# ScalarE's rounding copy of each dense weight half queued behind its first step for the next half

## The chip, the cores and the metric

The kernel runs on one core of a Trainium2 chip. The metric is the device time of one execution in microseconds (us). A core has TensorE (PE; PEld is its loading of weights), VectorE (DVE), ScalarE (ACT), GpSimd (POOL) and SyncE (SP), whose queue issues most of the transfers here. Each engine takes its own instructions in order, and semaphores tie the engines together.

## The reference, cut to what matters

Three layers on 2,304 tokens of width 512:

```python
# attention with random features: 4 batches, 8 heads, 576 tokens, head width 64, 128 features
h = x @ omega.T - sum(x*x)/2;  phi = exp(h - max(h)) / sqrt(m)        # for q and for k, scaled
num = phi_q @ (phi_k.T @ v);   den = phi_q @ sum(phi_k) + 1e-6;   x = num / den
# a dense layer: w_in is 512 x 2048, w_out is 2048 x 512
h = x @ w_in;  x = maximum(0.01*h, h) @ w_out
# eight experts, each token to the one with the largest logit
e = argmax(x @ w_gate);  out = gate * eom * (relu(x @ w1[e]) @ w2[e])
```

All of it is in 32-bit floats, except that `w_in` and `w_out` come in as 64-bit floats and are turned into 32-bit ones on the chip.

## The kernel before, in words

Each large product is made of three matmuls on numbers split in two: a high part, which is the value rounded to the type that TensorE multiplies fast (names ending in h: `xh`, `wih`, `woh`, `gh`), and a low part, the rest (`xl`, `wil`, `wol`, `gl`). The product is high by high, low by high, and high by low.

The tokens are cut into nine chunks of 256, the inner width of 2,048 into eight units of 256. `h_unit(c, u)` makes one unit of the hidden layer of chunk c (24 matmuls, lines 464 to 466), copies it out of PSUM (`g`, ScalarE line 469 and VectorE line 470) and splits it. `x_unit(c, u)` multiplies it with `w_out` (lines 483 to 485). Units of chunks 0 and 1 alternate. The attention items, in stages (`s_load` to `s_xt`), run ahead of the dense layer and then between its units: projection `pw` (line 291), row maxima and `bias` on VectorE (lines 303 to 312), `exp` on ScalarE (line 320), the sum over k (`kvp`, line 359, copied out by ScalarE as `kv`, line 374), transposes and `num` (lines 404 and 417), and the result `xr`, turned and split into `xh` and `xl`.

The dense weights come in 32 halves (`load_w`, line 174): for each unit u two of `w_in` and two of `w_out`, 512 KB each. A half is loaded into one of two `wraw` buffers (lines 184 and 196). ScalarE's **first step** (line 201) brings the upper word's exponent into range; three VectorE steps (lines 202 to 204) assemble the 32-bit float in `w32`, one of two buffers; ScalarE's **rounding copy** (line 209, in `hi_lo`) writes the high part; GpSimd's subtract (line 212) writes the low part. Eight halves (units 0 and 1) are loaded during the attention that goes ahead of the dense layer; the four of unit u+1 are asked for as chunk 0's unit u begins (line 829), for u from 1 to 6.

The order on each engine is set by a scheduler at build time: it simulates the program with estimated times, and takes from what is ready by priority, which is mostly the order in the text. `tc.issue_after(ins)` makes what is written in its block stand behind `ins` on the engine of `ins`. So one line that moves work can shift other instructions on every engine.

Of the kernel before, what the change touches and what calls it, by code (L numbers as in the profile page):

```python
# [11 lines left out]
F32 = mybir.dt.float32  # L12
# [3 lines left out]
AF = mybir.ActivationFunctionType  # L16
# [66 lines left out]
def f32(ap):  # L83
    return ap.bitcast(F32)
# [3 lines left out]
def tile_kernel(ctx: ExitStack, tc: tile.TileContext, kT, k_nat, v_nat, qT, q_nat, om, w_in, w_out, wg, w1, w2, out, stop=None, dbg=None):  # L88
    nc = tc.nc
# [45 lines left out]
    with ExitStack() as pa:  # L135
# [38 lines left out]
        def load_w(kind, u, half, pool):  # L174

            raw = pool.tile([P, 512, 2], I32, name="wraw", tag="wraw")
            if kind == "in":
                if win[u] is None:
                    wh = wring.tile([P, ND, 2 * P], F32R, name="wih", tag="w")
                    wl = wring.tile([P, ND, 2 * P], F32R, name="wil", tag="w")  # L180
                    win[u] = (wh, wl)
                wh, wl = win[u]
                with tc.issue_after(newest[-1]):
                    nc.sync.dma_start(raw.rearrange("p (i a) b -> p i (a b)", i=2),
                                      w_in[2 * half * P:2 * (half + 1) * P, u * 256:(u + 1) * 256].bitcast(I32).rearrange("(i p) a -> p i a", i=2))
                wh, wl = wh[:, 2 * half:2 * half + 2, :], wl[:, 2 * half:2 * half + 2, :]
                wh, wl = wh.rearrange("p a b -> p (a b)"), wl.rearrange("p a b -> p (a b)")
            else:
                if wout[u] is None:
                    wh = wring.tile([P, 2, D], F32R, name="woh", tag="w")  # L190
                    wl = wring.tile([P, 2, D], F32R, name="wol", tag="w")
                    wout[u] = (wh, wl)
                wh, wl = wout[u]
                f = 2 * u + half
                with tc.issue_after(newest[-1]):
                    nc.sync.dma_start(raw.rearrange("p a b -> p (a b)"), w_out[f * P:(f + 1) * P, :].bitcast(I32))
                wh, wl = wh[:, half, :], wl[:, half, :]
            top, low = raw[:, :, 1], raw[:, :, 0]
            w = pool.tile([P, 512], I32, name="w32", tag="w32")

            nc.scalar.activation(w.bitcast(F32), top.bitcast(F32), AF.Copy, scale=2.0 ** -112)
            nc.vector.tensor_scalar(w, w, 0x0FFFFFFF, 3, op0=ALU.bitwise_and, op1=ALU.logical_shift_left)
            nc.vector.scalar_tensor_tensor(w, top, -0x80000000, w, op0=ALU.bitwise_and, op1=ALU.bitwise_or)
            nc.vector.scalar_tensor_tensor(w, low, 29, w, op0=ALU.logical_shift_right, op1=ALU.bitwise_or)
            hi_lo(wh, wl, w.bitcast(F32), nc.scalar, nc.gpsimd)

        def hi_lo(dst_hi, dst_lo, src, hi_eng, lo_eng):
            if hi_eng is nc.scalar:
                nc.scalar.copy(dst_hi, src)
            else:  # L210
                hi_eng.tensor_copy(dst_hi, src)
            return lo_eng.tensor_sub(dst_lo, src, f32(dst_hi)).ins  # L212


        order = [(k, u, h) for u in range(NU) for k in ("in", "out") for h in range(2)]
        loaded = 0
# [238 lines left out]
        def h_unit(c, u):  # L455
            assert xdone.get(c) == CH * NH // 2, (c, u, xdone)
            hdone[c] = u + 1
            xh, xl = xT[c]
            hp = ps_h.tile([P, 2, CH], F32, name="hp", tag="h")
            wh, wl = win[u]  # L460
            for i in range(2):
                for d in range(ND):
                    a, b_ = wh[:, d, i * P:(i + 1) * P], wl[:, d, i * P:(i + 1) * P]
                    nc.tensor.matmul(hp[:, i, :], a, xh[:, d, :], start=d == 0, stop=False)  # L464
                    nc.tensor.matmul(hp[:, i, :], a, xl[:, d, :], start=False, stop=False)  # L465
                    nc.tensor.matmul(hp[:, i, :], b_, xh[:, d, :], start=False, stop=d == ND - 1)  # L466
            with tc.high_priority(offset=AHEAD):
                g = sb.tile([P, 2, CH], F32, name="g", tag="g", bufs=1)
                last_g[:] = [nc.scalar.copy(g, hp).ins]  # L469
                nc.vector.scalar_tensor_tensor(g, hp, 0.01, g, op0=ALU.mult, op1=ALU.max)  # L470
                gh = sb.tile([P, 2, CH], F32R, name="gh", tag="gh")
                gl = sb.tile([P, 2, CH], F32R, name="gl", tag="gl")
                last_g.append(hi_lo(gh, gl, g, nc.vector if c > 1 else nc.scalar, nc.vector))
            return gh, gl

        def x_unit(c, u, gg, acc):
            gh, gl = gg
            wh, wl = wout[u]
            for i in range(2):
                for t in range(2):  # L480
                    a, b_ = gh[:, i, t * P:(t + 1) * P], gl[:, i, t * P:(t + 1) * P]
                    h_, l_ = wh[:, i, :], wl[:, i, :]
                    nc.tensor.matmul(acc[t], a, h_, start=u == 0 and i == 0, stop=False)  # L483
                    nc.tensor.matmul(acc[t], a, l_, start=False, stop=False)  # L484
                    nc.tensor.matmul(acc[t], b_, h_, start=False, stop=u == NU - 1 and i == 1)  # L485
# [333 lines left out]
        for i, (c, u) in enumerate(pairs):  # L819

            rate = RATE
            for cc in range(c, NCH):
                left = [k + TAIL for k, it in enumerate(seq) if it[0] == cc] + [len(o) for c_, o in flow if c_ == cc]
                if left and hbeg.get(cc, 0) - 1 > i:
                    rate = max(rate, max(left) / (hbeg[cc] - 1 - i))
            if u == 0:
                at = [(ps_x, "x"), (ps_x, "x")] if c != 1 else [(ps_proj, "pj"), (ps_a, "a")]
                acc[c] = [ps.tile([P, D], F32, name=f"acc{t}", tag=tag) for t, (ps, tag) in enumerate(at)]
            while c == 0 and loaded < min(len(order), max(4 * (u + 2), WPRE + int(u * (32 - WPRE) / WU))):
                load_w(*order[loaded], wst)  # L830
                loaded += 1
            if i + 1 < len(pairs):
                gg[pairs[i + 1]] = h_unit(*pairs[i + 1])
            if c == NCH - 1 and u == 0:

                assert not flow and slot is not None
                pq.close()
                eo = ctx.enter_context(tc.tile_pool(name="eo", bufs=2, side="right", reuse_waits="tile"))
                block, second = Block(slot, 0), Block(slot, 1)
                block.rows()  # L840
                second.rows()
            owed += rate
            steps = int(owed)
            owed -= steps
            for k in range(steps + 1):
                if k == (steps + 1) // 2:
                    x_unit(c, u, gg.pop((c, u)), acc[c])
                if k == steps:
                    break
                if routes:  # L850
                    tick((-1, routes.pop(0)))
                elif seq and (seq[0][0] < 3 or i + int(6 / rate) >= hend.get(seq[0][0] - 2, 0)):
                    tick(seq.pop(0))
                else:
                    tick()
            if slot is None and c == NCH - 2 and not routes and not any(c_ < 0 for c_, _ in flow):
                slot = early()
                slot.fetch(0)
                slot.fetch(1)
            if c == NCH - 1:  # L860
                slot.split(u, last_g)
                if u == NU - 2:
                    for d in range(ND):
                        block.xt(d)
            if u < NU - 1:
                continue
            if c == 0:
                pads()
                gates()
            both_done[0] = c > 0  # L870
            rows = (wst if c == 1 else rt).tile([P, 2, ROW], F32, name="rows", tag="wraw" if c == 1 else "rows")
            nc.vector.memset(rows[:, :, D + 1:D + 2], 0.0)
            nc.scalar.copy(rows[:, 0, 0:D], acc[c][0])
            nc.vector.tensor_copy(rows[:, 1, 0:D], acc[c][1])
            routes.append(route_item(c, rows)[0])
# [138 lines left out]
```

## Time and profile before

| | |
|---|---|
| time, median of 3 runs | 862.88 us (862.8 to 868.14) |
| the profiled execution | 862.73 us, of which the span from the first to the last instruction is 861.0 us |
| busy in the span | PE 831.8 us (97%), DVE 450.7 (52%), ACT 306.5 (36%), POOL 176.1 (20%) |
| DVE busy by fortieths of the span, tenths | 6899788735555456445555444536644444243220 |
| TensorE clock granted, same slices | 9899899999999999999999999999999999999998 |

The 32 first steps start between 11.7 and 159.3 us, so the stretch in question is the first fifth of the span. The table shows averages over very different stages: what a change there is worth is read from the instructions for which TensorE waits in that stretch.

In the rows below, a row of the timeline gives the start, the duration, the engine, the line, the operation with its tiles as output<-inputs, and the number of instructions. The brackets tell how long the engine sat idle just before, and which instruction ended that.

### The profile page before, as it was taken

To read this page: it belongs to the slowest core of one execution; us is meant where nothing else is said; L and a number is where in the kernel's file an instruction comes from. 1 tells how busy PE (TensorE), PEld (TensorE's weight loads), DVE (VectorE), ACT (ScalarE), POOL (GpSimd) and SP (SyncE) were. 2 spreads that over 40 slices of the span, in tenths; PEclk is the share of its full clock that TensorE was granted. 3 is DMA by queue.
4 is the path that set the end of the run, shared out by engine and by line. 5 is a ranking of instruction groups with operands and counts; after the bars stand their busy time and mean duration, and the time that the engine had idled before them with its cause. 6 is when DMAs were issued, how large, how long until landed. Compare 5 with 4: busy or idle time off the path is not lost. (4 is left out here: it accounts for less than half of the span.)

```text
span 861.0 us, 13985 instructions
## 1 busy us (share of the span) xinstructions
PE 831.8 (97%) x5299; PEld 729.0 (85%) x5299; DVE 450.7 (52%) x1142; ACT 306.5 (36%) x755; POOL 176.1 (20%) x253
## 2 busy tenths in 40 slices
PE   9889988999999999999999999999999999999996
PEld 7768776788889988988889989898889789887894
DVE  6899788735555456445555444536644444243220
ACT  4666556434333323333333213214333334232210
POOL 3545544400122011112101010021003221120001
PEclk9899999899999999999999999999999999999998
DMA  7636655301443003133101000042505554151001
GB/s 230 208 120 185 190 179 166 124 10 31 60 81 102 26 26 56 46 71 76 43 27 24 2 25 2 10 121 74 98 26 179 177 155 123 59 172 50 7 25 33
DMA packets 46153, 73.55 MB, mean 85 GB/s; under 512 B 6017, under 2 KB 28673, under 8 KB 46082
## 3 DMA queue, kind: packets, MB, share of 16 engines
q1 hardware_dynamic: 42562, 63.14, 26.5%
q0 software_dynamic: 3520, 9.47, 3.5%
q8 instruction: 44, 0.72, 0.4%
q14 instruction: 27, 0.22, 0.1%
HBM read 62.00 MB, written 10.59 MB: 84 GB/s over the span
## 5 line engine op out<-in xcount | busy, mean ns | idle before, releaser
L464 PE MATMUL hp<-xh,wih 128*128 128x256 f32 x576 | 166.3, 289 | 2.3 <-DVE xl L212 2.0
L465 PE MATMUL hp<-xl,wih 128*128 128x256 f32 x576 | 161.8, 281 | 0.1
L466 PE MATMUL hp<-xh,wil 128*128 128x256 f32 x576 | 161.6, 281 | 0.0
L483 PE MATMUL acc<-woh,gh 128*128 128x512 f32 x288 | 123.0, 427 | 1.3 <-ACT kv L374 1.3
L320 ACT ACTIVATE h<-pw,bias 128x128 f32<-128x128 f32 x288 | 84.8, 372 | 105.7 <-DVE bias L312 81.5
L470 DVE SCALAR_TENSOR_TENSOR g<-hp,g 128x512 f32<-128x512 f32 x72 | 49.6, 689 | 135.8 <-ACT g L469 123.6
L485 PE MATMUL acc<-woh,gl 128*128 128x512 f32 x288 | 115.5, 402 | 0.0
L484 PE MATMUL acc<-wol,gh 128*128 128x512 f32 x288 | 114.3, 397 | 0.0
L464 PEld LDWEIGHTS hp<-xh,wih 128*128 128x128 f32 x576 | 108.8, 189 | 5.7 <-issue 2.4
L465 PEld LDWEIGHTS hp<-xl,wih 128*128 128x128 f32 x576 | 108.8, 189 | 2.1 <-DVE xl L212 0.3
L466 PEld LDWEIGHTS hp<-xh,wil 128*128 128x128 f32 x576 | 108.7, 189 | 0.0
L469 ACT COPY g<-hp 128x512 f32<-128x512 f32 x72 | 42.3, 587 | 138.3 <-PE hp L466 138.2
L723 PE MATMUL eht<-exh,ewh 128*128 128x256 f32 (+1 forms) x256 | 75.9, 296 | 0.0
L724 PE MATMUL eht<-exl,ewh 128*128 128x256 f32 (+1 forms) x256 | 75.6, 295 | 0.0
L725 PE MATMUL eht<-exh,ewl 128*128 128x256 f32 (+1 forms) x256 | 75.5, 295 | 0.0
L291 PE MATMUL pw<-om_raw,xpair 128*128 128x256 f32 (+1 forms) x260 | 71.8, 392 | 2.6 <-ACT h L320 2.6
L271 POOL TENSOR_TENSOR nat<-nat 128x256 f32<-128x256 f32 (+1 forms) x65 | 44.9, 693 | 135.9 <-DMA nat<-k_nat 58.8
L485 PEld LDWEIGHTS acc<-woh,gl 128*128 128x128 f32 x288 | 54.4, 189 | 12.7 <-DVE gl L212 0.5
L483 PEld LDWEIGHTS acc<-woh,gh 128*128 128x128 f32 x288 | 54.2, 188 | 12.5 <-ACT kv L374 1.7
L741 PE MATMUL eyt<-ewh,ehh 128*128 128x512 f32 (+1 forms) x160 | 64.6, 404 | 0.0
L727 DVE SCALAR_TENSOR_TENSOR ehl<-eht,ehh 128x256 fp32r<-128x256 f32 (+1 forms) x64 | 29.1, 456 | 67.2 <-ACT ehh L726 64.3
L742 PE MATMUL eyt<-ewl,ehh 128*128 128x512 f32 (+1 forms) x160 | 63.3, 395 | 0.0
(157 smaller groups left out, 1475.1 us busy)
## 6 DMA issues: line engine op xcount, KB each, us to landing
eraw<-w SPq DMA_DIRECT2D x32, 512.0 KB, 3.6
wraw<-w_in SPq DMA_DIRECT2D x16, 512.0 KB, 5.1
wraw<-w_out SPq DMA_DIRECT2D x16, 512.0 KB, 3.9
x_d<-rows SPq DMA_DIRECT2D x9, 514.0 KB, 8.9
xpair<-qT SPq DMA_DIRECT2D x18, 256.0 KB, 2.9
nat<-q_nat SPq DMA_DIRECT2D x30, 128.0 KB, 2.8
nat<-k_nat SPq DMA_DIRECT2D x27, 128.0 KB, 2.2
xpair<-kT SPq DMA_DIRECT2D x12, 256.0 KB, 6.2
```

The source lines that it names most:

```text
L291: nc.tensor.matmul(pj[:, 2 * j:2 * j + k // HD, :], st["raw"][0:k, j * P:(j + 1) * P], om_raw[0:k, 0:M * k // HD], start=True, stop=True)
L320: nc.scalar.activation(h[:, j, :], src[:, j // 2, j % 2], AF.Exp, bias=bias[:, j:j + 1], scale=sc)
L464: nc.tensor.matmul(hp[:, i, :], a, xh[:, d, :], start=d == 0, stop=False)
L465: nc.tensor.matmul(hp[:, i, :], a, xl[:, d, :], start=False, stop=False)
L466: nc.tensor.matmul(hp[:, i, :], b_, xh[:, d, :], start=False, stop=d == ND - 1)
L483: nc.tensor.matmul(acc[t], a, h_, start=u == 0 and i == 0, stop=False)
L484: nc.tensor.matmul(acc[t], a, l_, start=False, stop=False)
L485: nc.tensor.matmul(acc[t], b_, h_, start=False, stop=u == NU - 1 and i == 1)
L723: nc.tensor.matmul(t, wh, self.xh[:, d, 0:n], start=d == 0, stop=False)
L724: nc.tensor.matmul(t, wh, self.xl[:, d, 0:n], start=False, stop=False)
L725: nc.tensor.matmul(t, wl, self.xh[:, d, 0:n], start=False, stop=d == ND - 1)
L741: nc.tensor.matmul(t, a, wh, start=f == 0, stop=False)
```

## The change

Before, each `load_w` ended with the rounding copy and the subtract of its own half. Now it puts them on a list (`owing`), and the next `load_w` writes them right behind its own first step, with `issue_after`, so that on ScalarE the copy of half k stands behind the first step of half k+1. After the last half, a call in the main loop writes what is still owed. No instruction is added or removed, no buffer or transfer is changed.

```diff
-            nc.scalar.activation(w.bitcast(F32), top.bitcast(F32), AF.Copy, scale=2.0 ** -112)
+            first_ = nc.scalar.activation(w.bitcast(F32), top.bitcast(F32), AF.Copy, scale=2.0 ** -112).ins
+
+            parts_of_last(first_)
             nc.vector.tensor_scalar(w, w, 0x0FFFFFFF, 3, op0=ALU.bitwise_and, op1=ALU.logical_shift_left)
             ...
-            hi_lo(wh, wl, w.bitcast(F32), nc.scalar, nc.gpsimd)
+            owing.append((wh, wl, w.bitcast(F32)))
+
+        owing = []
+
+        def parts_of_last(after=None):
+            while owing:
+                with ExitStack() as order_:
+                    if after is not None:
+                        order_.enter_context(tc.issue_after(after))
+                    hi_lo(*owing.pop(0), nc.scalar, nc.gpsimd)
             ...
                 load_w(*order[loaded], wst)
                 loaded += 1
+            if c == 0 and loaded == len(order):
+                parts_of_last()
```

What the scheduler makes of it is seen in the engines' queues. In the changed kernel all lines behind 205 stand 11 to 13 lower in the file (209 is 220, 212 is 223, 320 is 331, 374 is 385, 469 is 480, 470 is 481), and the numbers of the tiles are smaller by two (`w_733` is `w_731`). Of the 32 halves, 16 had their copy behind the next half's first step already; for 15 the two now change places, and the last is as it was.

The first place is the end of the attention that goes ahead of the dense layer, at the first `g`. ScalarE's queue there before:

```order
L209 CAST woh<-w_733 128x512
L469 COPY g<-hp 128x512
L320 ACTIVATE h<-pw,bias 128x128 x4
L209 CAST gh<-g 128x512
L320 ACTIVATE h<-pw,bias 128x128 x4
L469 COPY g<-hp 128x512
L201 ACTIVATE w_904<-wraw 128x512
```

and now:

```order
L480 COPY g<-hp 128x512
L331 ACTIVATE h<-pw,bias 128x128 x4
L220 CAST gh<-g 128x512
L331 ACTIVATE h<-pw,bias 128x128 x4
L480 COPY g<-hp 128x512
L201 ACTIVATE w_902<-wraw 128x512
L220 CAST woh<-w_731 128x512
```

The copy of the eighth half has gone from ahead of the first `g` to behind the second `g` and the ninth half's first step. On VectorE at the same place, before:

```order
L303 TENSOR_REDUCE mx<-pw 128x2x2
L156 CAST wgo<-wg_raw 128x4x16
L310 SCALAR_TENSOR_TENSOR ngm<-mx,s_829 128x4
L470 SCALAR_TENSOR_TENSOR g<-hp,g 128x512
L312 TENSOR_TENSOR bias<-ngm,s_829 128x4
```

and now:

```order
L314 TENSOR_REDUCE mx<-pw 128x2x2
L481 SCALAR_TENSOR_TENSOR g<-hp,g 128x512
L321 SCALAR_TENSOR_TENSOR ngm<-mx,s_827 128x4
L283 TENSOR_REDUCE ssq<-nat 128x4
L323 TENSOR_TENSOR bias<-ngm,s_827 128x4
L156 CAST wgo<-wg_raw 128x4x16
```

The step for `g` now stands ahead of the cast of the gate's weights (`wgo`).

The second place is ScalarE around the last half of unit 3 (`w_1119`), before:

```order
L209 CAST woh<-w_1119 128x512
L469 COPY g<-hp 128x512
L374 COPY kv_1159<-kvp 128x132
L320 ACTIVATE h<-pw,bias 128x128 x3
L209 CAST gh<-g 128x512
L320 ACTIVATE h<-pw,bias 128x128
L201 ACTIVATE w_1310<-wraw 128x512
```

and now:

```order
L331 ACTIVATE h<-pw,bias 128x128 x7
L480 COPY g<-hp 128x512
L385 COPY kv_1157<-kvp 128x132
L201 ACTIVATE w_1308<-wraw 128x512
L220 CAST woh<-w_1117 128x512
L220 CAST gh<-g 128x512
```

The copies of `g` and `kv` no longer stand behind the copy of this half.

The third place is ScalarE around the second `w_in` half of unit 5 (`w_1534`), before:

```order
L201 ACTIVATE w_1534<-wraw 128x512
L209 CAST wih<-w_1525 128x512
L209 CAST wih<-w_1534 128x512
L320 ACTIVATE h<-pw,bias 128x128 x2
L469 COPY g<-hp 128x512
L201 ACTIVATE w_1545<-wraw 128x512
L374 COPY kv_1159<-kvp 128x132
L320 ACTIVATE h<-pw,bias 128x128
```

and now:

```order
L201 ACTIVATE w_1532<-wraw 128x512
L220 CAST gh<-g 128x512
L331 ACTIVATE h<-pw,bias 128x128 x4
L220 CAST wih<-w_1523 128x512
L201 ACTIVATE w_1543<-wraw 128x512
L220 CAST wih<-w_1532 128x512
L480 COPY g<-hp 128x512
L385 COPY kv_1157<-kvp 128x132
```

All four `exp` of that item now stand ahead of both copies. Elsewhere, GpSimd's subtract for `w_381` stands behind two more squares (`nat`) and two more small scalings than before, the `exp` of the item behind the last half of unit 5 stand behind the next half's first step (`w_1789`), and `kv` at the last half of unit 4 stands ahead of three `exp` which it used to follow. From the time at which the last dense weights are split on, the queues of all engines are as before.

## Rows read from the trace of the kernel before

**Rows 1.** Stretches: us, busy PE, PEld, DVE, ACT, POOL; granted clock, DMA share, GB/s.

```profile
20.00:180.00 160.00, 141.87 (x883) 120.18 (x882) 132.55 (x298) 93.40 (x237) 76.42 (x89) 0.96 0.52 161
180.00:840.00 660.00, 658.18 (x4253) 584.13 (x4252) 304.35 (x804) 202.88 (x489) 89.32 (x141) 1.00 0.25 64
33.00:39.70 6.70, 6.64 (x29) 6.18 (x29) 4.80 (x15) 4.44 (x16) 2.45 (x4) 0.51 0.63 175
```

**Rows 2.** Waits, 0 to 200 us: engine, line <- what for; us in total, times, longest.

```profile
ACT wih L209 <- DVE w L204: 18.4, 13, 2.7
...
ACT woh L209 <- DVE w L204: 10.7, 11, 2.4
```

**Rows 3.** Timeline of PE: stalls between 20 and 131 us.

```profile
21.41 1.21 PE L359 MATMUL kvp<-vgroup,h 128*128 128x66 f32 x8 [0.44 <-ACT h L320]
...
33.06 0.48 PE L404 MATMUL qtp<-ident,h 128*128 128x128 f32 x1 [2.47 <-ACT h L320]
...
56.80 1.11 PE L417 MATMUL nump<-kv,et 128*128 128x66 f32 x8 [1.00 <-DVE g L470]
...
94.46 0.50 PE L483 MATMUL acc<-woh,gh 128*128 128x512 f32 x1 [1.34 <-ACT kv L374]
...
108.79 0.49 PE L359 MATMUL kvp<-vb,h 128*128 128x132 f32 x2 [1.97 <-ACT kv L374]
...
124.18 1.11 PE L291 MATMUL pw<-om_raw,xpair 128*128 128x256 f32 x4 [1.39 <-ACT h L320]
...
130.22 1.11 PE L291 MATMUL pw<-om_raw,xpair 128*128 128x256 f32 x4 [0.50 <-ACT h L320]
```

**Rows 4.** Timeline of ACT at those stalls.

```profile
20.47 0.62 ACT L209 CAST wih<-w 128x512 fp32r<-128x512 f32 x1 [1.00 <-DVE w L204]
...
53.94 0.58 ACT L469 COPY g<-hp 128x512 f32<-128x512 f32 x1
...
93.13 0.62 ACT L209 CAST woh<-w 128x512 fp32r<-128x512 f32 x1 [2.40 <-DVE w L204]
...
94.14 0.27 ACT L374 COPY kv<-kvp 128x132 f32<-128x132 f32 x1
...
106.62 0.66 ACT L201 ACTIVATE w<-wraw 128x512 f32<-128x512 f32 x1 [2.89 <-DMA wraw<-w_out]
...
108.45 0.28 ACT L374 COPY kv<-kvp 128x132 f32<-128x132 f32 x1
...
120.73 0.62 ACT L209 CAST wih<-w 128x512 fp32r<-128x512 f32 x1 [2.69 <-DVE w L204]
...
123.72 0.41 ACT L320 ACTIVATE h<-pw,bias 128x128 f32<-128x128 f32 x1
...
129.29 0.88 ACT L320 ACTIVATE h<-pw,bias 128x128 f32<-128x128 f32 x3
130.05 0.68 ACT L201 ACTIVATE w<-wraw 128x512 f32<-128x512 f32 x1
```

**Rows 5.** Timeline of DVE around 32 and 55 us.

```profile
31.73 0.87 DVE L312 TENSOR_TENSOR bias<-ngm,s 128x4 f32<-128x4 f32 x1
...
33.20 0.15 DVE L312 TENSOR_TENSOR bias<-ngm,s 128x4 f32<-128x4 f32 x1
...
54.29 1.31 DVE L156 CAST wgo<-wg_raw 128x64 fp32r<-128x64 f32 x1
...
56.06 0.68 DVE L470 SCALAR_TENSOR_TENSOR g<-hp,g 128x512 f32<-128x512 f32 x1
```

**Rows 6.** Timeline of POOL: a subtract for `w_out`, and one for `w_in`.

```profile
31.32 1.26 POOL L212 TENSOR_TENSOR wol<-w,woh 128x512 fp32r<-128x512 f32 x1
...
67.85 1.31 POOL L212 TENSOR_TENSOR wil<-w,wih 128x512 fp32r<-128x512 f32 x1 [1.62 <-ACT wih L209]
```

**Rows 7.** ACT and PE around unit 2 of chunk 0, from their timelines.

```profile
67.68 0.67 ACT L201 ACTIVATE w<-wraw 128x512 f32<-128x512 f32 x1
...
69.91 0.28 PE L466 MATMUL hp<-xh,wil 128*128 128x256 f32 x1
```

## The prediction, as it was recorded

> **What bounds the kernel now.** I read the busy time by stretch first, then the waits, then the timelines of TensorE and of the engine that each of its stalls names. From 180 us on TensorE is busy 658.18 us of 660 at the full clock [rows 1]: nothing is to be had there, and what the change wins or loses before 180 us only moves the rest. Between 20 and 180 us TensorE is busy 141.87 of 160 us, so 18.1 us are idle, and its granted clock is 0.96 in the mean, which loses another 0.04 x 160 = 6.4 us. These 24.5 us are all that any order of the other engines could win. VectorE is busy 132.55 us there: it is nearly full, and the change takes nothing off it. ScalarE, busy 93.40 us, is not full but blocked: it stood 18.4 + 10.7 = 29.1 us, 24 times, at the rounding copy of a half, until VectorE had finished that half [rows 2]. What counts is not these 29.1 us but what stood behind such a copy while TensorE waited for it.
>
> **What the change does.** It removes and adds no instruction. The new order turns copy and next first step round for 15 of 32 halves; for 16 they stood so already. Nothing is moved past a transfer's issue by it: a `wraw` buffer comes free with VectorE's last step, which does not wait for the copy. The two buffers of `w32` still suffice, since the copy of half k is written before half k+2 asks for its buffer. What the change costs by itself is that the copy of half k, and with it GpSimd's subtract, now waits for the load of half k+1. The gains and losses, place by place:
>
> 1. At 21 us TensorE waits 0.44 us for `exp` [rows 3], which stood behind the copy that ScalarE started at 20.47 after waiting 1.00 us [rows 4]. That copy now comes behind these `exp` and the next first step, and it takes more than 0.44 us (0.62). **-0.44.**
> 2. At 30.59 TensorE stops for 2.47 us until an `exp` [rows 3]. That `exp` waits for `bias`, which ran 0.87 us [rows 5] while GpSimd subtracted `w_381` from 31.32 to 32.58 [rows 6]; the next `bias`, with no subtract beside it, took 0.15 [rows 5]. That subtract is now later. The bounds are 0 (another operation of GpSimd runs there) and -0.72. I take the row: **-0.72.**
> 3. At 55.80 TensorE waits 1.00 us for VectorE's `g` [rows 3], which ran from 56.06 to 56.74. It now stands ahead of the `wgo` cast, which started at 54.29 [rows 5]. Its input, ScalarE's copy `g`, ended at 53.94 + 0.58 = 54.52 [rows 4] and can only be earlier without the rounding copy ahead of it. So `g` ends by 54.52 + 0.68 = 55.20, before TensorE gets there. **-1.00.** Next late is `xr`, as before.
> 4. At 93.1 TensorE waits 1.34 us for `kv` [rows 3], copied at 94.14 behind a rounding copy that had waited 2.40 us, until 93.13 [rows 4]. `kv` now stands ahead of that copy. **-1.34.**
> 5. At 106.8 TensorE waits 1.97 us for `kv` [rows 3]. ScalarE had waited 2.89 us for a load, until 106.62, and did three `exp` and a rounding copy before `kv` at 108.45 [rows 4]. Now `kv` stands ahead of the `exp`, behind the first step and one copy: 106.62 + 0.66 + 0.62 = 107.90 at the latest, by the full durations. **-0.55.** The wait for the load stays.
> 6. At 122.8 TensorE waits 1.39 us for the last `exp` of an item, which ended at 123.72 + 0.41 = 124.13 [rows 3, 4]. It stood behind two rounding copies, of which the second waited 2.69 us. All four `exp` now stand ahead of both. **-1.39.**
> 7. Against it: at unit 2 of chunk 0 the copy of the second `w_in` half must wait for the first step at 67.68, which ends at 68.35; copy 0.62 and subtract 1.31 then end at 70.28, and TensorE wants `wil` at 69.91 [rows 7, 6]. **+0.37.** The other 14 copies have longer before their use: the program asks for those weights one unit of the other chunk earlier.
> 8. At 130.2 the `exp` that TensorE waits for started at 129.29; they now stand behind a first step that ran at 130.05 [rows 4] because of its load. They would start at 130.05 + 0.68 = 130.73, 1.44 us later. **+1.44**, if the load is no earlier than before.
>
> The sum is -0.44 - 0.72 - 1.00 - 1.34 - 0.55 - 1.39 + 0.37 + 1.44 = **-3.63 us**. All other stalls I leave as they are. The profiled execution took 862.73 us, the median is 862.88; -3.63 on the latter gives **859.2 us**.
>
> On term 2 the Trainium skill (GPSIMD Engine Reference, Specifications) says that GpSimd shares its way into SBUF with VectorE, and that they contend where a VectorE instruction reads two inputs from SBUF. By that rule the subtract, put elsewhere, stretches another instruction of a nearly full VectorE, and term 2 would be lost again: 860.0 instead of 859.2. No run so far shows where it falls, so the sum keeps the row's 0.72.
>
> **The bounds.** At most the 24.5 us come back, and no row supports most of that. On the other side, each of the 15 copies now depends on a load that was later than its first step by up to 2.89 us [rows 4].
>
> **The rivals.**
>
> *The stalls come back elsewhere.* VectorE is busy 83% of the stretch and orders its own work almost as before. TensorE then waits for VectorE's next result where it no longer waits for ScalarE, and terms 1 to 6 (5.44 us) are mostly given back. For it: half of the copies were in the new order already. Against it: terms 3, 4 and 6 end at an instruction of which the inputs were ready well before. With a fifth of the 5.44 us kept and the costs of terms 7 and 8 paid, it is 862.88 - 1.09 + 1.81 = 863.6, so 862 to 865. Chance 0.27.
>
> *The clock stays up.* After the stop of 2.47 us at 30.59 the granted clock is 0.51 from 33 to 39.7 us, the lower level of 1.2 GHz [rows 1]. If the stop is short enough, now that terms 1 and 2 shorten what leads to it, TensorE gains at most half of 6.7 us, 3.3 us, and with it VectorE, which then waited for it. 859.2 - 3.3 = 855.9, and with a second such stretch spared 854 or below. Against it: a stop of 2.47 - 0.72 us is still long, and one of 1.97 us at 106.8 did not bring the clock down, so I cannot say where it turns. Chance 0.17.
>
> *Slower: the weights come late.* The place is `h_unit` of chunk 0, units 2 to 7. The copy of the second `w_in` half stands behind the first step of the first `w_out` half, hence behind its load; if that load comes as late as the longest wait in the rows, 2.89 us, the copy, the subtract and TensorE's `wil` slip by that, and ScalarE, held there, holds back `exp`, `g` and `kv` too. Unit 2 has nothing to spare (term 7). With three of the six units hit, 3 x 2.89 = 8.7 us, and the time is 859.2 + 8.7 = 867.9. It decides where the first step starts over 1 us later than before. Against it: of the three first steps in the rows two ran with no wait for a load [rows 4, 7], and the buffers come free no later. Chance 0.12; in a third to half of it the gains are lost as well, and the time is over 871.5.
>
> The Trainium skill (TensorE: Matmul & The Clock Gate, Architectural detail) says that ScalarE's queue is a strict first-in, first-out; by that a blocked first step lets nothing pass, which is this last rival's mechanism, and the wait of 2.89 us with `exp` and `kv` behind it [rows 4] agrees.
>
> **How the numbers follow.** The forecast, a gain of 1 to 6.5 us around 859.2, has what is left, 0.44. One in ten is left out on either side: the range runs from 853, with the clock spared twice, to 866.5, which takes in the stalls that come back and half of the slower case. A measurement of this kernel tells about 1% from no change, 8.6 us. Faster by over 1% is below 854.3: most of the better half of the clock case and a little of the forecast's tail, 0.11. Slower by over 1% is above 871.5: 0.05. The rest, 0.84, is within 1%.
>
> **What the changed profile would show.** The waits of ScalarE at the rounding copies should fall from 29.1 us by about half, to those at copies whose order stays. TensorE's idle time from 20 to 180 us should fall from 18.1 to about 14.5, the stalls at `g` near 56, at `kv` near 93 and at `exp` near 124 should be gone, and a small one on `wil` should stand in unit 2. Everything behind 180 us should look the same, some 3.6 us earlier. I am wrong if ScalarE often waits for `wraw` loads as it did at 106.62 and TensorE's matmuls of `h_unit` wait for `wil`, if the idle time of TensorE stays near 18 us with other names behind it, or if the clock rows at 33 to 40 us have changed.

## The result, and the profile after

The changed kernel takes 873.97 us (median of 6 executions, 870.64 to 876.24); the kernel before, with three more executions, 862.96. The ratio is 1.0111, with a 95% interval of 1.0086 to 1.0137: slower by about 1%. The prediction was 859.2, with a range of 853.0 to 866.5. It was wrong in size and in sign.

The profiled execution after took 874.99 us, 12.26 more than that of before. The nine stores of `rows` (one for each chunk of tokens, issued by SP) show where these 12.26 us are lost, since all engines' queues hold the same work in the same order from the first of them on:

| store of `rows` | 1 | 4 | 5 | 6 | 7 | 8 | 9 |
|---|---|---|---|---|---|---|---|
| issued, before (us) | 221.00 | 379.90 | 449.43 | 507.59 | 558.26 | 596.29 | 634.09 |
| issued, after (us) | 222.76 | 382.26 | 453.88 | 513.12 | 563.81 | 608.53 | 646.35 |
| later by | 1.76 | 2.36 | 4.45 | 5.53 | 5.55 | 12.24 | 12.26 |

So in these two executions the stretch that the change touches lost 1.76 us, where I had forecast a gain of 3.63. All the rest, 10.5 us, was lost where the prediction said that nothing would change, and 6.7 of it between the 7th and the 8th store. One execution each is little to go by for the smaller steps: a second profile of the changed kernel (after2, below) issued its first store at 220.19, ahead of the kernel before, and its 5th 69.36 us behind its 4th, against 69.53 before and 71.62 here. Between its 7th and 8th it lost 5.3 us. The early loss is therefore judged by medians, further down. The stretches of the two kernels (us, busy PE, PEld, DVE, ACT and POOL, granted clock, DMA share, GB/s), before and then after:

```profile
20.00:100.00 80.00, 69.96 (x442) 60.14 (x442) 72.28 (x169) 52.18 (x138) 41.24 (x52) 0.96 0.57 174
100.00:180.00 80.00, 71.91 (x443) 60.04 (x441) 60.27 (x130) 41.23 (x99) 35.18 (x37) 0.96 0.47 148
...
380.00:420.00 40.00, 39.56 (x257) 34.75 (x256) 19.56 (x53) 11.85 (x35) 8.69 (x17) 1.00 0.34 74
...
560.00:600.00 40.00, 40.00 (x270) 35.95 (x269) 18.69 (x48) 10.13 (x19) 8.36 (x11) 1.00 0.33 102
```

```profile
20.00:100.00 80.00, 71.15 (x452) 60.87 (x450) 75.26 (x167) 51.50 (x134) 42.80 (x52) 0.96 0.56 174
100.00:180.00 80.00, 68.11 (x425) 56.71 (x425) 64.94 (x132) 41.56 (x102) 34.61 (x38) 0.98 0.49 149
...
20.00:180.00 160.00, 139.26 (x874) 117.57 (x873) 140.20 (x297) 93.06 (x236) 77.41 (x89) 0.97 0.53 162
...
380.00:420.00 40.00, 39.08 (x245) 34.03 (x244) 17.98 (x59) 12.03 (x38) 7.87 (x17) 0.96 0.34 77
...
560.00:600.00 40.00, 35.73 (x221) 31.09 (x220) 15.30 (x46) 6.52 (x13) 7.36 (x10) 0.91 0.25 77
```

TensorE is idle 160 - 139.26 = 20.7 us between 20 and 180, against 18.1 before [rows 1]: 1.2 us less up to 100 us, 3.8 more behind it. VectorE is busy 7.65 us longer there, with as many instructions. Between 560 and 600 TensorE, which was always busy before, is idle for 4.3 us, and its clock falls to 0.91 in the mean.

**The late loss.** VectorE's timeline at the 7th store, before and after (start, duration, engine and line, operation, and in brackets the idle time ahead of it and what ended that):

```profile
561.20 0.69 DVE L470 SCALAR_TENSOR_TENSOR g<-hp,g 128x512 f32<-128x512 f32 x1 [1.91 <-ACT g L469]
561.84 0.06 DVE L872 MEMSET rows<- 128x2 f32 x1
561.92 0.43 DVE L211 CAST gh<-g 128x512 fp32r<-128x512 f32 x1
```

```profile
566.75 0.69 DVE L481 SCALAR_TENSOR_TENSOR g<-hp,g 128x512 f32<-128x512 f32 x1 [1.60 <-ACT g L480]
573.64 0.42 DVE L222 CAST gh<-g 128x512 fp32r<-128x512 f32 x1 [6.20 <-issue]
573.67 0.06 DVE L885 MEMSET rows<- 128x2 f32 x1
```

TensorE's timeline there, after:

```profile
574.12 0.79 PE L494 MATMUL acc<-woh,gh 128*128 128x512 f32 x1 [4.27 <-DVE gh L222]
```

The page calls VectorE's 6.20 us "issue", a wait for nothing that it knows. What ended is at the start of the next row: the memset of `rows` and `gh` begin together. `rows` has one buffer here, so the memset for the next chunk must wait until the store of this one has landed, and it stands between `g` and `gh` in VectorE's queue. Before, it began 561.84 - 558.26 = 3.58 us behind the store's issue; now 573.67 - 563.81 = 9.86. A store is moved by 16 DMA engines, and the trace has records of when their parts landed: in the 7th store all but one of those recorded are in 3.07 us behind the issue, the last at 9.80. One part came 6.7 us behind the others, and the memset began 0.06 us after it. The DMA queues from 563.8 to 565.9 us show what stood beside it:

```profile
q1 hardware_dynamic: 214, 0.44, 55.8%
q14 instruction: 1, 0.01, 2.3%
```

A block of 8 KB of instructions was fetched, 1.03 us behind the store's issue. In the same stretch of the kernel before no instruction queue has a packet; the block that I take for VectorE's (the experiments tell why) came at 554.36, ahead of the store.

**The early loss.** ScalarE's waits up to 200 us after:

```profile
ACT h L331 <- DVE bias L323: 20.7, 15, 2.5
...
ACT h L331 <- DVE ngm L321: 6.6, 1, 6.6
...
ACT wih L220 <- DVE w L206: 5.6, 4, 2.7
...
ACT woh L220 <- DVE w L206: 3.7, 3, 1.7
...
ACT w L201 <- POOL wil L223: 2.3, 2, 1.4
ACT w L201 <- POOL wol L223: 2.1, 3, 0.9
```

At the copies it now waits 9.3 us instead of 29.1 [rows 2]; at `exp` 27.3 instead of 18.5. The wait has changed its name. The last two lines are new: ScalarE's first step waits, 4.4 us in five waits, for GpSimd's subtract, which still reads the `w32` buffer that the step wants. TensorE's stalls, which answer to [rows 3]:

```profile
21.08 0.95 PE L370 MATMUL kvp<-vgroup,h 128*128 128x66 f32 x6 [0.42 <-ACT h L331]
...
27.90 1.21 PE L370 MATMUL kvp<-vgroup,h 128*128 128x66 f32 x8 [1.50 <-ACT h L331]
...
93.86 0.50 PE L494 MATMUL acc<-woh,gh 128*128 128x512 f32 x1 [1.54 <-ACT h L331]
...
102.78 1.13 PE L302 MATMUL pw<-om_raw,xpair 128*128 128x256 f32 x4 [2.19 <-ACT h L331]
...
108.94 0.49 PE L370 MATMUL kvp<-vb,h 128*128 128x132 f32 x2 [0.64 <-ACT kv L385]
...
126.04 1.11 PE L302 MATMUL pw<-om_raw,xpair 128*128 128x256 f32 x4 [1.91 <-ACT h L331]
```

The one of 2.19 us at 102.78, which is new, can be followed back over three engines, GpSimd, VectorE and ScalarE:

```profile
99.73 1.45 POOL L223 TENSOR_TENSOR wil<-w,wih 128x512 fp32r<-128x512 f32 x1 [1.28 <-ACT wih L220]
```

```profile
99.97 1.23 DVE L323 TENSOR_TENSOR bias<-ngm,s 128x4 f32<-128x4 f32 x1
```

```profile
101.58 1.14 ACT L331 ACTIVATE h<-pw,bias 128x128 f32<-128x128 f32 x4 [1.94 <-DVE bias L323]
```

`bias` took 1.23 us instead of 0.15 [rows 5] and ended when the subtract did (101.18 and 101.20), and `exp` waited for it.

### The profile page after: what moved, and what is told of

It reads as the page before. It is cut to its first block, busy times and chain, and to the rows that moved or that the text cites. A ratio compares the mean times of both kernels' runs of the same rounds, so it can differ in the third digit from the quotient of the medians.

```text
span 873.3 us, 13973 instructions
## 1 busy us (share of the span) xinstructions
PE 835.3 (96%) x5299; PEld 730.5 (84%) x5299; DVE 456.1 (52%) x1142; ACT 307.0 (35%) x755; POOL 177.7 (20%) x253
## 5 line engine op out<-in xcount | busy, mean ns | idle before, releaser
L495 PEld LDWEIGHTS acc<-wol,gh 128*128 128x128 f32 x288 | 55.1, 191 | 10.0
```

## The experiments

Each is an edit of the kernel before or of the changed one. The times are medians; the ratio is to the kernel before, run on the same chip (862.1 to 862.6 us there), with its 95% interval. b_pad, a_pad5, a_loop and b_subdve ran on one chip, the others on another.

| kernel | what it is | us | ratio | interval |
|---|---|---|---|---|
| after2 | the changed kernel again | 869.99 | 1.0090 | 1.0069 to 1.0112 |
| a_rows | changed, memset moved | 863.79 | 1.0016 | 1.0000 to 1.0032 |
| b_rows | before, memset moved | 862.60 | 1.0004 | 0.9988 to 1.0020 |
| a_pad | changed, 24 memsets more | 865.96 | 1.0045 | 1.0024 to 1.0066 |
| a_pad5 | changed, 5 memsets more | 866.03 | 1.0033 | 1.0013 to 1.0053 |
| b_pad | before, 124 memsets more | 871.85 | 1.0116 | 1.0072 to 1.0160 |
| a_nosub | a_rows, no subtract | 850.00 | 0.9867 | 0.9837 to 0.9898 |
| b_nosub | b_rows, no subtract | 848.17 | 0.9846 | 0.9819 to 0.9873 |
| a_pro | a_rows, new order for 8 halves | 861.50 | 0.9988 | 0.9969 to 1.0006 |
| a_loop | a_rows, new order for the other 24 | 863.51 | 1.0008 | 0.9991 to 1.0025 |
| a_sublate | a_rows, subtract still later | 863.10 | 1.0008 | 0.9994 to 1.0023 |
| b_subdve | b_rows, subtract on VectorE | 856.22 | 0.9921 | 0.9895 to 0.9947 |
| a_subdve | a_rows, subtract on VectorE | 859.31 | 0.9965 | 0.9948 to 0.9981 |
| a_pro_dve | a_pro, subtract on VectorE | 855.55 | 0.9933 | 0.9910 to 0.9955 |

### Is it the memset behind the store? a_rows and b_rows

```diff
-            nc.vector.memset(rows[:, :, D + 1:D + 2], 0.0)
             nc.scalar.copy(rows[:, 0, 0:D], acc[c][0])
-            nc.vector.tensor_copy(rows[:, 1, 0:D], acc[c][1])
+            copied = nc.vector.tensor_copy(rows[:, 1, 0:D], acc[c][1]).ins
+            with tc.issue_after(copied):
+                nc.vector.memset(rows[:, :, D + 1:D + 2], 0.0)
```

a_rows: 

> The changed kernel, with VectorE's memset of `rows` put behind its copy of the accumulator. Theory 1 (a store that lands late: VectorE's memset waits for the store of the chunk before it and stands ahead of `gh`, which TensorE needs; this costs about 2.7 us at 392 and 6.7 us at 573, the stretches at half the clock included): 873.97 - 9.4 = 864.6, between 863.5 and 866.5, with VectorE's pauses of 6.46 and 6.23 us gone. Rival 1 (VectorE lacks instructions there, whatever comes next): a pause of 4 to 6 us stays ahead of another instruction of VectorE, and the time is 871 to 875.

b_rows: 

> The kernel before, with the same memset put behind the copy. Theory 1: its pause of 5.77 us at 389 goes, which cost TensorE about 0.4 us: 862.5, between 861.5 and 863, and none of its executions at 868 to 870. Rival 1: 862.9, with such executions among them still.

a_rows came out at 863.79, where theory 1 put it, 10 us below the changed kernel; b_rows at 862.60, no different from the kernel before. Nothing of VectorE's work was taken away, and in a_rows TensorE is busy without a gap in both stretches:

```profile
380.00:420.00 40.00, 40.00 (x259) 35.18 (x259) 20.15 (x55) 11.88 (x36) 8.38 (x18) 1.00 0.37 78
560.00:600.00 40.00, 40.00 (x272) 36.05 (x271) 19.89 (x49) 9.61 (x20) 7.77 (x10) 1.00 0.33 96
```

At the 4th store (first row) this is the work of the memset's move alone: in a_rows that store's last part lands 10.46 us behind its issue, as late as in the changed kernel. At the 7th (second row) two things changed at once. The moved memset brings five more waits into VectorE's queue, and there the fetch now begins 4.83 us ahead of the store, which lands in 3.12 us. So the 10 us are what both are worth together; the next experiments take them apart. Against rival 1 stands this: in these traces and those of the next section the last part of a store came over 8 us behind its issue ten times with the memset in its old place, and each time the memset began 0.05 to 0.06 us after that part. VectorE waited for the landing.

### Why does the store land late? after2, a_pad, a_pad5 and b_pad

The memsets of the pads write one column that nobody reads. In a_pad and a_pad5 they stand at the start of VectorE's queue; the order on the other engines is that of the changed kernel, name by name. In b_pad they stand behind the copy of chunk 1's accumulator, and run between 200 and 243 us, earlier than I had meant.

```diff
-        owed = 0.0
+        owed = 0.0; pad = const.tile([P, 1], F32, name="pad")
...
+            if (c, u) == (5, 3): [nc.vector.memset(pad, 0.0) for k in range(24)]
             rate = RATE
```

and in b_pad, beside the same tile:

```diff
+            copied = nc.vector.tensor_copy(rows[:, 1, 0:D], acc[c][1]).ins
+            if c == 1:
+                with tc.issue_after(copied):
+                    for k in range(124):
+                        nc.vector.memset(pad, 0.0)
```

after2: 

> The changed kernel once more, unchanged. Theory 1 (a store of `rows` that lands late while VectorE's memset stands ahead of `gh`, because a fetch of instructions meets the store): the place of the fetch is fixed by the program, so the pause of 6.23 us at 573 comes again and the time is 870.5 to 876.5. Rival (chance of that chip or execution): 863.5 to 866.

a_pad: 

> The changed kernel with 24 memsets of one column more at the start of VectorE's queue, nothing else moved on any engine. Theory 1: VectorE's instructions are fetched 8 KB at a time, and the fetch that now begins 1.03 us behind the store issued at 563.89 comes about 20 instructions of VectorE earlier, ahead of the store; the store lands in 3.5 to 4 us, the pause of 6.23 us goes, and the time is 865 to 868.5. Rival (the pause belongs to the order or to the place in the program, not to the meeting of fetch and store): 870.5 to 876.5, with the pause still there.

a_pad5: 

> The changed kernel with 5 memsets of one column at the start of VectorE's queue, nothing else moved. Theory 1: with 5 instructions more the fetch falls ahead of `lg` again, as in the kernel before; the store issued near 559 lands in 3.5 to 4 us, no pause of VectorE stands there, and the time is 864 to 867. Rival: 869 to 875, as without them.

b_pad: 

> The kernel before with 124 memsets of one column in VectorE's queue between 240 and 350 us, where VectorE is half idle. Theory 1 (the changed kernel is slow at 573 because VectorE's queue holds 4 instructions less ahead of the routing step `lg`, so that the fetch of its next 128 falls behind `lg` and meets the store): 124 more are 4 less in steps of 128, so the fetch falls behind `lg` here too, about 1 us behind the store issued near 558; the store lands 8.5 to 10 us after its issue, VectorE pauses 5 to 6.5 us ahead of `gh`, and the kernel before becomes 866.5 to 870.5. Rival (that pause is the changed order's): 862 to 864, with the store landing in 3.5 to 4 us.

The pause comes again in after2 (5.18 us ahead of `gh`; the time is 0.5 us below the bound that I gave). With 24 memsets more, and with 5, it is gone. VectorE in a_pad5, where the store was issued at 561.67:

```profile
564.61 0.69 DVE L481 SCALAR_TENSOR_TENSOR g<-hp,g 128x512 f32<-128x512 f32 x1 [1.92 <-issue]
565.25 0.06 DVE L885 MEMSET rows<- 128x2 f32 x1
565.34 0.43 DVE L222 CAST gh<-g 128x512 fp32r<-128x512 f32 x1
```

The memset starts 3.58 us behind the issue, as in the kernel before. Both times, 865.96 and 866.03, came out where theory 1 had them, but are still 3.8 us above the kernel before: the early loss is in them, and from the 4th store, late in them too, to the 5th they take 70.23 and 71.21 us, where the kernel before took 69.53. And 124 memsets make the kernel before as slow as the changed one (871.85; I had allowed 866.5 to 870.5). VectorE in b_pad, with the store issued at 560.19:

```profile
563.12 0.69 DVE L470 SCALAR_TENSOR_TENSOR g<-hp,g 128x512 f32<-128x512 f32 x1 [1.61 <-ACT g L469]
569.01 0.42 DVE L211 CAST gh<-g 128x512 fp32r<-128x512 f32 x1 [5.20 <-issue]
569.03 0.06 DVE L872 MEMSET rows<- 128x2 f32 x1
```

From the 7th store to the 8th b_pad takes 44.23 us, 6.2 more than the kernel before. Not all of its loss is that: the memsets themselves held TensorE up, and from the 1st store to the 3rd b_pad takes 93.99 us instead of 89.88.

```profile
236.03 0.63 PE L526 MATMUL lgp<-rth,wgo 128*32 128x256 f32 x4 [3.50 <-DVE pad L878]
```

So the pause at the 7th store is neither the changed order nor the work, but the place of VectorE's instructions in its stream. The trace records 943 of them ahead of this chunk's first routing step `lg` before, 939 after, 944 in a_pad5 and in a_rows: the new order needs 4 instructions less, all of them waits. Before, the fetches of this queue that keep step with VectorE came at its records 561, 696, 816 and 943, one block of 8 KB for some 127 records. With 943 or 944 ahead the last of these falls while VectorE waits for `lg`; with 939 it falls within the burst of short routing steps behind `lg`, at the end of which the store is issued: 26 records behind `lg` in after, in after2 and in b_pad. In the 7th store the fetch begins 1.03 us behind the issue after, 1.02 in after2, 1.03 in b_pad, and each time one part lands at 8.8 to 9.8 us. In a_pad the fetch has moved to the 5th store, 0.93 us behind its issue, and there the last part lands at 8.31, the one before at 3.55. In the sixteen traces of this case no other store has a recorded part later than 5.5 us, apart from the 2nd and the 4th, which have loads of the next chunk beside them. Where no such fetch starts in the 2.5 us behind an issue, the 4th store apart, the memset started 3.45 to 4.1 us behind it.

A fetch soon behind the issue is not enough, though. In b_subdve, a_subdve and a_pro_dve (below) one begins 0.63 to 0.64 us behind the 7th store's issue, and the last part recorded lands at 3.18 to 3.94. In all these traces the first packet of the 5th and of the 7th store starts 0.89 to 0.90 us behind the issue: the three harmless fetches began ahead of it, the four harmful ones 0.04 to 0.14 us behind it. What that does to a part is not shown. Another suspect falls: GpSimd stores a small table (`tab_d`) beside each of these stores, but its 64 packets begin 2.4 to 3.0 us behind the issue whether the store is late or not.

The 4th store is another matter: it lands 8.7 to 11.4 us behind its issue in every trace, the kernel before among them, mostly with several parts late. A fetch of 8 KB begins 1.0 to 1.4 us behind its issue in twelve of the sixteen; in a_pad and the three kernels named above none does, and it is as late (10.2 to 11.4). There VectorE paused 5.74 us before and 6.44 after; it cost TensorE 0.44 us before, and after 0.92 and a clock of 0.96.

Why one part waits 4.8 to 6.7 us more than the others is not settled. The Trainium skill (DMA: Bandwidth & Descriptors, Queues, rings and completion order) says that the write that counts a part as done lands only after every earlier write of the same DMA engine, whichever queue it came from. By that a fetch can hold up a store's completion, not only its data; but the records don't tell which DMA engine carried what, so no run here shows it.

### Is the early loss the subtract beside VectorE? a_nosub, b_nosub, a_sublate

a_nosub and b_nosub leave out the low parts of the dense weights: in place of `wil` and `wol` TensorE multiplies with `wih` and `woh` once more.

```diff
-                    wl = wring.tile([P, ND, 2 * P], F32R, name="wil", tag="w")
+                    wl = wh
...
-                    hi_lo(*owing.pop(0), nc.scalar, nc.gpsimd)
+                    dst_, _, src_ = owing.pop(0)
+                    nc.scalar.copy(dst_, src_)
```

a_nosub: 

> a_rows without GpSimd's subtract of the dense weights (the lower part is the upper part once more, so one operation for each half is left out). Theory 2 (the subtract of one half now runs beside VectorE's three steps of the next and stretches them by 6.4 us from 20 to 200 us): VectorE's busy time there is within 1 us of b_nosub's, and the time is 2 to 4 us below b_nosub. Rival 2 (the new order itself costs, exp standing behind first steps that wait for loads): 1 to 2.5 us above b_nosub.

b_nosub: 

> b_rows without GpSimd's subtract of the dense weights, the partner of a_nosub. Theory 2: VectorE's busy time from 20 to 200 us falls by 2 us or less, since the subtract ran beside little of VectorE's work that it slows; 860 to 862.5. Rival 2: the same.

a_sublate keeps the subtract and lets it wait for one more step of VectorE:

```diff
+            third_ = nc.vector.scalar_tensor_tensor(w, low, 29, w, op0=ALU.logical_shift_right, op1=ALU.bitwise_or).ins
+            while lower:
+                d_, s_, h_ = lower.pop(0)
+                with tc.issue_after(third_):
+                    nc.gpsimd.tensor_sub(d_, s_, f32(h_))
```

a_sublate: 

> a_rows with GpSimd's subtract of a half put behind VectorE's third step of the next half instead of behind ScalarE's copy alone. Theory 2 (a subtract that runs beside VectorE's steps stretches them, and that is what the changed order loses): VectorE's three steps fall back to means of about 0.47 and 0.82 us, and the time is 861 to 862.5. Rival 2 (the subtract stretches whatever stands beside it, and the weights come later): 863.5 to 866.

The stretching is real. VectorE's three steps and the two small operations of `bias`, after (line, count, busy us, mean ns):

```profile
L205 DVE SCALAR_TENSOR_TENSOR w<-wraw,w 128x512 int32<-128x512 int32 x32 | 29.7, 928 | 0.2
...
L206 DVE SCALAR_TENSOR_TENSOR w<-wraw,w 128x512 int32<-128x512 int32 x32 | 27.5, 860 | 0.1
...
L321 DVE SCALAR_TENSOR_TENSOR ngm<-mx,s 128x4 f32<-128x4 f32 (+1 forms) x74 | 19.2, 261 | 0.8
...
L323 DVE TENSOR_TENSOR bias<-ngm,s 128x4 f32<-128x4 f32 (+1 forms) x74 | 17.8, 240 | 1.6
...
L204 DVE TENSOR_SCALAR w<-w 128x512 int32<-128x512 int32 x32 | 17.5, 547 | 1.9 <-ACT w L201 1.8
```

The three steps take 74.7 us after; before they took 68.2 (means of 468, 881 and 782 ns), and without the subtract 60.7 (476, 696 and 725). But theory 2 said more, that this is what the new order loses, and there it fails: without the subtract the changed order is still 1.8 us slower than the old one (four executions each), and a_sublate didn't bring the steps down (539 ns, and 906 in the mean of the other two). Its 863.10 lies in neither of its ranges, and is no different from a_rows. What I had not expected at all is what the subtract costs in either order, some 14 us, for an operation that runs on an engine with time to spare: b_nosub came out 12 us below its range, and VectorE's busy time from 20 to 200 us fell by 8.4 us (140.44 in b_rows, 132.07 in b_nosub), not by 2 or less.

### Where in the program is it lost? a_pro and a_loop

```diff
             owing.append((wh, wl, w.bitcast(F32)))
+            if dense[0]:
+                parts_of_last()
```

(a_loop has `if not dense[0]`.)

a_pro: 

> a_rows with the new order only for the halves loaded ahead of the first h_unit (8 of 32); in the loop the copy follows its own three steps as before. Theory 3 (the new order gains before 90 us and loses 3.4 us between 90 and 112 us): 1 to 1.6 us below b_rows, 861 to 861.7. Rival (the loss belongs to the first halves, whose copies fall behind first steps that wait for loads): 863.5 to 864.5.

a_loop: 

> a_rows with the new order only for the halves loaded in the loop, the partner of a_pro. Theory 3 (the loss of the new order is made in the loop): 1 to 2.5 us above b_rows, 863.5 to 865. Rival (it needs both parts, or is scatter): within 0.7 us of b_rows.

Both came out where theory 3 had them: 861.50 and 863.51. The intervals of the two overlap, so this is a lean and not a proof; the first store of `rows` is issued at 219.48 in a_pro, 221.65 in a_loop, 221.09 in a_rows and 219.56 in b_rows, in one profiled execution each. By this the loss lies in the loop, where the weights are loaded beside chunk 0's dense layer.

### With the subtract on VectorE: b_subdve, a_subdve, a_pro_dve

```diff
-            hi_lo(wh, wl, w.bitcast(F32), nc.scalar, nc.gpsimd)
+            hi_lo(wh, wl, w.bitcast(F32), nc.scalar, nc.vector)
```

and the same last argument in the other two.

b_subdve: 

> b_rows with the subtract of the dense weights on VectorE instead of GpSimd. Theory 4 (what the subtract costs is mostly VectorE held beside GpSimd): VectorE does 30 more instructions of 0.69 us, 20.7 us, and is no longer stretched, some 12 us; the time is 857 to 862. Rival (VectorE is the bound of the stretch from 20 to 180 us, and its sum is up by 9 us): 864 to 870.

a_subdve: 

> a_rows with the subtract of the dense weights on VectorE, so the changed order with nothing of GpSimd's beside VectorE's three steps. Theory 2 (the order loses in the loop because the subtract then falls beside those steps and stretches them): without it the order loses nothing, and its time is at most that of b_subdve, 854 to 856.3. Rival 2 (the loss is the order's own: exp, g and kv stand behind first steps, and copies behind loads): 857.5 to 859.

a_pro_dve: 

> a_pro with the subtract of the dense weights on VectorE: the new order for the first 8 halves alone. If what the first halves gain (0.6 us, from a_pro) adds to what the subtract on VectorE gains: 855.6, between 854.5 and 856.5, the fastest of all. Rival (with VectorE no longer held, those copies have nothing left to gain): 856.2 to 857.5.

b_subdve is faster than both kernels of this case, 856.22, and 0.8 us better than theory 4 had allowed. VectorE's rows in it:

```profile
L203 DVE SCALAR_TENSOR_TENSOR w<-wraw,w 128x512 int32<-128x512 int32 x32 | 22.1, 689 | 0.1
...
L204 DVE SCALAR_TENSOR_TENSOR w<-wraw,w 128x512 int32<-128x512 int32 x32 | 21.8, 681 | 0.0
...
L202 DVE TENSOR_SCALAR w<-w 128x512 int32<-128x512 int32 x32 | 14.0, 438 | 3.7 <-ACT w L201 3.6
...
L212 DVE TENSOR_TENSOR wol<-w,woh 128x512 fp32r<-128x512 f32 x16 | 11.7, 731 | 0.6 <-ACT woh L209 0.5
...
L212 DVE TENSOR_TENSOR wil<-w,wih 128x512 fp32r<-128x512 f32 x16 | 11.6, 724 | 0.8 <-ACT wih L209 0.8
```

VectorE does 32 instructions more, 23.3 us, and its three steps take 57.9 us instead of 68.2, `ngm` and `bias` 28.0 instead of 36.4: 18.7 us come back. From 20 to 180 us VectorE is busy 134.98 us, 2.4 more than before [rows 1], while TensorE does 145.97 - 141.87 = 4.1 us more. With nothing of GpSimd's beside VectorE, a_subdve's steps are as short (441, 712 and 681 ns) and at 859.31 it is still 3.1 us slower than b_subdve, 0.3 above what rival 2 had allowed. The two ran on different chips; their intervals against the kernel before only just fail to meet. This speaks against theory 2 and for rival 2: the loss is the order's own. a_pro_dve, at 855.55, is the fastest, but by less than can be told from b_subdve. It ran on the chip of a_subdve, differs from it only in the halves of the loop, and is 3.8 us faster; that too puts the loss in the loop.

## Why the prediction was wrong

**The step that failed** is "Everything behind 180 us should look the same, some 3.6 us earlier". The work there is the same, and its order too, but not its instruction stream: 4 instructions less of VectorE's move a fetch into a store. Of the 11.0 us between the medians 1.2 are left in a_rows, so this step cost 9.8 us, and 6.7 by after2 (7.9 above the kernel before on its chip). Between the 7th and 8th store alone it is 6.7 us in the profile after, 5.3 in after2 and 6.2 in b_pad. It was luck that in the kernel before that store landed in time, and its own rows could have warned: VectorE pauses 5.74 us at 389, called "issue", at the same memset. I read a TensorE that is busy 658.18 us of 660 [rows 1] as a stretch that nothing can disturb. It was one that a late store, 6 us long, had not yet hit at a place where TensorE needs the next result.

**The sum was wrong as well.** With the memset out of the way the order costs 1.2 us (a_rows against b_rows) where I forecast -3.63. The intervals of these two overlap; that it costs something rests on the same sign in the other two pairs, 1.8 and 3.1 us. By its terms, in the profile after:

- Term 1 (0.44 us at 21) did not come: 0.42 us for the same `exp` stand there still. Term 2 came at its place: the `bias` there took 0.15 us, with no subtract beside it, and the stop of 2.47 us is gone. But the stall ahead of it, 0.98 us at 27.16 before, is 1.50 at 27.90, and one of 0.94 stands at 35.92, while the subtract holds an `ngm` for 1.15 us. In the sum 1.0 us is won.
- Term 3 came at its place: no stall at `nump` near 56. But 0.56 us for the next `g` stand at 57.51.
- Term 4 (1.34 us for `kv` at 93) was paid under another name: 1.54 us for `exp`. Term 5 came, 1.97 to 0.64, but 2.19 us for `exp` stand 6 us ahead of it. Term 6 (1.39 at 124) did not: 1.91 us for `exp` at 126.
- Terms 7 and 8, the costs, did not come as put: there is no stall for `wil` on TensorE in unit 2, and none of 0.5 us at 131.

What I named as the mechanism, ScalarE blocked at the copies, was there, and the waits at them fell to a third. But "All other stalls I leave as they are" was the wrong step in the sum: behind a copy that no longer waits comes an `exp` whose `bias` is late. This is the first rival, "the stalls come back elsewhere", which I priced at 863.6 and gave 0.27; a_rows measured 863.79. That the number fits so well is luck in part, since the rival counts in terms 7 and 8.

The prediction also held that two buffers of `w32` suffice, since the copy is written in time. It left out that the subtract reads the same buffer: before, no first step waits for one; after, they wait 4.4 us for it. What this costs TensorE no run shows by itself.

**The rule I set aside.** For term 2 I kept the row's 0.72 us against the Trainium skill (GPSIMD Engine Reference, Specifications), by which GpSimd shares its way into SBUF with VectorE. The trace after agrees with that rule: a subtract found another `bias` to hold, which reads two inputs, 1.23 us instead of 0.15, and VectorE's steps became 6.5 us longer in sum. (A step with one input was held as well, as the last section shows. The same row of the Trainium skill names, beside two inputs, a mode of VectorE with two ports; no run shows which mode that step ran in.) I should have taken the whole cost of the subtract from the rows, not the one instance of it at 31 us; yet the runs without GpSimd's subtract show that this is not what makes the new order slower.

**The slower rival**, weights that come late, priced at 867.9, has the wrong mechanism for this loss: the changed kernel's TensorE has no wait for `wil` over 0.3 us, and ScalarE's waits for loads up to 200 us rose from 6.4 to 8.7 us, none longer than 2.2.

**The clock rival** did not come in the profiled execution: from 28 to 45 us the granted clock is 0.80 in the mean before and after. In a_rows it is 0.90.

**Open:** which of the order's waits costs the 1.2 to 3.1 us in the loop. In a_subdve TensorE waits for `wih` at 69.42 and 106.38, 0.61 and 0.67 us, which b_subdve does not; the rest is spread over small stalls and over stretches at 1.2 GHz that differ from execution to execution.

## What to carry to other kernels

Look for instructions that wait for a store to land and stand ahead of what the critical engine needs: a pause called "issue" in front of a memset or of a buffer's first write is such a wait, and it may be cheap only by chance of time. An edit that is worth under 1% should be judged with such places taken out in both kernels, or a few instructions of padding will decide the comparison. And an operation put on an idle engine isn't free when it stretches its neighbour: moving the subtract from GpSimd, which had time, to VectorE, which was busy 83% of the stretch, gained 0.8%.

## What the runs showed of the hardware

- In four stores of 514 KB a fetch of 8 KB of instructions began 0.93 to 1.03 us behind the issue, just behind the store's first packet, and one of the 16 parts landed at 8.3 to 9.8 us, where the others recorded landed by 3.6 us. In three, one began at 0.63 to 0.64 us, ahead of the first packet, and all recorded parts landed by 3.9 us.
- Five memsets of 0.06 us, put some 560 us ahead, removed that delay; 124 of them brought it into a kernel that did not have it.
- TensorE, busy without a gap before, stopped for 4.27 us until 574.12; from 572.2 to 578.8 us its granted clock was 0.50, the lower level of 1.2 GHz:

```profile
572.20:578.80 6.60, 4.68 (x11) 3.67 (x12) 2.92 (x6) 0.59 (x1) 1.18 (x2) 0.50 0.23 59
```

- A 128x4 operation of VectorE beside a 128x512 subtract of GpSimd ended with the subtract: 1.23 us instead of 0.15. A 128x512 step with one input did nearly the same, 1.47 us from 90.30 beside a subtract from 90.21 to 91.50, where one alone takes 0.41.
